# Query copies and probability scaling on GpSimd, with a re-fitted order table, in a recurrent memory transformer block

## The chip, the cores and the metric

The kernel runs on one core of one Trainium2 chip. The core has a TensorE (PE in the profile, with its weight loads listed apart as PEld), a VectorE (DVE), a ScalarE (ACT), a GpSimd (POOL) and a SyncE (SP) that issues the DMAs. The metric is the device time of one execution in microseconds; lower is better. The kernel before was timed three times.

## The reference

One block with two residual branches. The first is attention with 32 heads of 128 over segments of 32 tokens, in which every segment also carries 8 memory rows. The memory rows' output of a segment is the memory input of the next one, so the 64 segments form a chain. The second is a gelu MLP from 512 to 1792 and back.

```python
def _A_ref(x, mem0, Wq, Wk, Wv, Wo, seg_len):       # x: 2048 x 512
    mem = mem0                                      # 8 x 512
    for s in range(n_seg):                          # 64 segments, one after the other
        h = concat([mem, x[segment s]])             # 40 rows
        q, k, v = h @ Wq, h @ Wk, h @ Wv            # 32 heads of 128
        scores = (q @ k.T) * scale
        scores = where((idx[:, None] < M) | (idx[:, None] >= idx[None, :]), scores, -1e9)
        o = (softmax(scores) @ v) @ Wo
        mem = o[:M]                                 # the next segment needs it
        outs.append(o[M:])

h = x + _A_ref(_layernorm(x), mem0, Wq, Wk, Wv, Wo, 32)
out = h + gelu(_layernorm(_layernorm(h)) @ w1 + b1) @ w2 + b2
```

## The kernel before

**Recording and planning.** The kernel doesn't write its instructions in their final order. `build_kernel` records operations (`S.op`, `S.either`, `S.dma`) with what they read and write and with a duration. `Sched.schedule` then gives every operation a start by a table of costs: `HOP` is the time between the end of an operation and the start of one that depends on it, `OVERLAP` is how far two neighbours on an engine may overlap, `SWITCH` is the price of a change of the PE's tile mode. Each operation's rank is the longest path behind it, plus a number from the table `BONUS` (by the tile that it writes and the place of its segment). `S.either` leaves the engine open: the planner takes the engine that ends first. On DVE, ACT and POOL the start times so found fix the order of the instructions, and on these in-order engines everything waits behind an instruction that waits.

**The PE's own order** is written out by hand. `ORDERS` lists, for each place, which units of which part come when: `Q0.0.2` is units 0 and 1 of the part Q0. Places are a1 to a3 (the first segments), m0 to m3 (segments 4 to 59, by their number modulo 4, 14 of each) and z60 to z63. `TURNED` says which passes walk their four 128-column chunks backwards; two passes that meet on the same chunk keep the loaded weights (`matmul_kept`).

**One segment.** In the matrix products the segment's rows are the PE's weights (128 by 32, four of them side by side) and the big weight matrices stream past, 512 columns at a time. A *unit* is four such matmuls.

- K0, K1, Q0, Q1, V0, V1 (line 796, or 547 with kept weights): four units each. The number is the half of the heads. K and Q leave PSUM as `kq` (ACT or DVE, lines 814 and 815) and are transposed on DVE (line 839) into `KALL` and `QT`. `q_seg` then copies the memory rows' queries from `QT` into `ZC` (line 853), and `qb_fill` adds queries of the tokens' extra rows from `QTB` (line 861, POOL).
- SC0, SC1 (line 963): the scores of the memory rows, from `ZC` and `KALL`. Their softmax is `nmc` (maximum, DVE, line 972), `EC` (exponential, ACT, 976), `rsc` (DVE, 979), `PC` (scaling, DVE, 982), `PTC` (transpose, DVE, 983).
- PV0, PV1 (lines 994 and 998): the memory rows' probabilities times V, in another tile mode. PVA (line 1055): the same for the tokens of the segment before.
- SA (line 1025): the tokens' scores. Their softmax is `nma`, `SA`, exponential, `sma`, `rsa` (1035 to 1039), `PA` (scaling with `rsa`, DVE, line 1042), `PTA` (transpose, DVE, line 1044). PVA of the next segment needs `PTA`.
- WO (line 1083): the output product, eight units. Its result is transposed on DVE (`TT`, line 1095) and its memory rows are added into `hT` (line 1089), which Q, K and V of the next segment read. This is the recurrence.
- F0, F1: work that doesn't hang on the recurrence and fills the PE: K, Q and V of extra rows of later blocks (`hB`), in m3 the eight units of `wo_B` (line 1112), near the end the first part of the MLP. `warm` units (line 765) take their place in the first segments.

After segment 63 the MLP runs (lines 1451 and 1465), with `p2_res` on POOL (line 1190) and `p2_norm` on DVE (line 1184). `align` inserts idle weight loads (pads) so that every fourth segment starts at the same place of the PE's instruction stream.

The lines around the change, with their numbers in the profile:

## Time and profile before

| | |
|---|---|
| timed, median of 3 | 807.47 us (805.72 to 808.97) |
| profiled execution, from its first to its last instruction | 802.2 us |
| difference of the two, which the profile doesn't show | 5.3 us |
| PE busy | 775.9 us (97%) |
| DVE busy | 600.7 us (75%) |
| ACT busy | 558.0 us (70%) |
| POOL busy | 90.1 us (11%) |
| granted PE clock, mean | 0.998 |

The first 60 us load the weights (16 MB), the segments run from about 43 to 705 us, the MLP ends the program. PE matmuls overlap in the profile: each row has its own length, and four stand side by side in the array. What a unit costs is therefore read from the distance of its start to the next unit's start, and "busy" is an upper bound on it. "Idle before" of PEld is time in which no weights were loaded, which costs nothing while the matmuls in the array keep it full.

### The profile page before, as it was taken

To read this page: it belongs to the slowest core of one execution; us is meant where nothing else is said; L and a number is where in the kernel's file an instruction comes from. 1 tells how busy PE (TensorE), PEld (TensorE's weight loads), DVE (VectorE), ACT (ScalarE), POOL (GpSimd) and SP (SyncE) were. 2 spreads that over 40 slices of the span, in tenths; PEclk is the share of its full clock that TensorE was granted. 3 is DMA by queue.
4 is the path that set the end of the run, shared out by engine and by line. 5 is a ranking of instruction groups with operands and counts; after the bars stand their busy time and mean duration, and the time that the engine had idled before them with its cause. 6 is when DMAs were issued, how large, how long until landed. Compare 5 with 4: busy or idle time off the path is not lost.

```text
span 802.2 us, 46835 instructions
## 1 busy us (share of the span) xinstructions
PE 775.9 (97%) x21699; PEld 423.1 (53%) x20880; DVE 600.7 (75%) x1847; ACT 558.0 (70%) x1580; POOL 90.1 (11%) x211
## 2 busy tenths in 40 slices
PE   2899999999999999999999999999999999999998
PEld 1455555555555555555555555555555555644444
DVE  3277878888888888888888888888888888732311
ACT  1557777777777777777778777777777777773342
POOL 5022000010001010101010101000000000020700
PEclk9999999999999999999999999999999999999999
DMA  9961010201111121102010202010212112074300
GB/s 367 394 174 24 4 37 11 45 12 37 26 33 30 30 33 27 36 19 42 19 43 15 49 12 50 13 37 20 50 25 56 51 38 59 17 232 127 86 27 26
DMA packets 65555, 48.77 MB, mean 61 GB/s; under 512 B 28996, under 2 KB 63308, under 8 KB 63820
## 3 DMA queue, kind: packets, MB, share of 16 engines
q1 hardware_dynamic: 65024, 45.50, 20.3%
q8 instruction: 166, 2.72, 1.4%
q14 instruction: 33, 0.27, 0.1%
q10 hardware_dynamic: 332, 0.27, 0.1%
HBM read 31.08 MB, written 8.13 MB: 49 GB/s over the span
## 4 chain that ended last, share of the span: by engine, by line
PE 91%; DMA 3%; DVE 2%; ACT 1%; SPq 1%; issue 1%; POOL 0%; DVEq 0%; ACTq 0%
PE ps L796 43%; PE ps L1083 15%; PE ps L547 8%; PE quad L1465 6%; PE ps L1451 5%; DMA WQ<-in_A_Wq_dram 3%; PE ps L1112 3%; PE quad L994 3%; PE quad L1055 2%; PE ps L1025 2%; PE ps L1233 1%; PE ps L963 1%; PE quad L963 1%; SPq L708 1%; PE quad L998 1%
## 5 line engine op out<-in xcount | busy, mean ns | idle before, releaser
L1083 PE MATMUL ps<-WO,OT 128*32 128x256 bf16 x4224 | 140.6, 274 | 0.1
L796 PE MATMUL ps<-WQ,hT 128*32 128x512 bf16 x1864 | 131.6, 379 | 0.7 <-DVE hT L1089 0.5
L796 PE MATMUL ps<-WV,hT 128*32 128x512 bf16 x1364 | 125.2, 381 | 0.0
L796 PE MATMUL ps<-WK,hT 128*32 128x512 bf16 x1700 | 123.6, 380 | 0.1
L815 ACT ACTIVATE kq<-ps 128x512 bf16<-128x512 f32 x160 | 95.4, 597 | 32.3 <-PE ps L796 26.4
L1083 PEld LDWEIGHTS ps<-WO,OT 128*32 128x32 bf16 x4224 | 100.9, 96 | 26.5 <-ACT OT L814 5.5
L814 ACT CAST kq<-ps 128x512 bf16<-128x512 f32 x162 | 94.8, 585 | 19.9 <-PE ps L796 13.1
L814 ACT CAST OT<-quad 128x128 bf16<-128x128 f32 x191 | 84.4, 442 | 27.0 <-PE quad L998 18.8
L839 DVE STREAM_TRANSPOSE KALL<-kq 128x256 f32<-128x256 f32 x160 | 71.2, 445 | 15.0 <-ACT kq L814 11.8
L796 PEld LDWEIGHTS ps<-WQ,hT 128*32 128x32 bf16 x1864 | 50.3, 97 | 58.8 <-issue 19.0
L861 POOL COPY ZC<-QTB 128x256 bf16<-128x256 bf16 x64 | 25.6, 401 | 477.2 <-PE ps L963 455.7
L796 PEld LDWEIGHTS ps<-WK,hT 128*32 128x32 bf16 x1700 | 45.8, 96 | 56.9 <-issue 14.5
L547 PE MATMUL ps<-WV,hT 128*32 128x512 bf16 x684 | 67.6, 379 | 0.0
L796 PEld LDWEIGHTS ps<-WV,hT 128*32 128x32 bf16 x1364 | 38.4, 97 | 47.3 <-issue 36.6
L839 DVE STREAM_TRANSPOSE QT<-kq 128x256 f32<-128x256 f32 x128 | 57.0, 445 | 6.5 <-ACT kq L815 1.9
L1454 ACT ACTIVATE WQ<-ps,b1t 128x512 bf16<-128x512 f32 x42 | 28.9, 688 | 46.6 <-PE ps L1451 46.6
L1095 DVE STREAM_TRANSPOSE TT<-ps 128x256 f32<-128x256 f32 x66 | 29.7, 450 | 36.3 <-PE ps L1083 36.1
L814 ACT CAST VS<-ps 128x512 bf16<-128x512 f32 x65 | 38.1, 586 | 26.6 <-PE ps L796 26.5
L814 DVE CAST VS<-ps 128x512 bf16<-128x512 f32 x63 | 41.8, 663 | 5.4 <-PE ps L796 5.4
L1541 DVE TENSOR_TENSOR WV<-quad,WV 128x512 bf16<-128x512 f32 (+1 forms) x16 | 10.5, 672 | 45.6 <-PE quad L1465 45.6
L982 DVE TENSOR_TENSOR PC<-EC,rsc 128x128 bf16<-128x128 f32 x128 | 39.7, 310 | 4.3
L1112 PE MATMUL ps<-WO,OTB 128*32 128x512 bf16 x512 | 42.1, 381 | 0.4 <-issue 0.2
(163 smaller groups left out, 1432.1 us busy)
## 6 DMA issues: line engine op xcount, KB each, us to landing
WV<-in_A_Wv_dram SPq DMA_DIRECT2D x4, 1024.0 KB, 8.5
WK<-in_A_Wk_dram SPq DMA_DIRECT2D x4, 1024.0 KB, 14.2
WQ<-in_A_Wq_dram SPq DMA_DIRECT2D x4, 1024.0 KB, 24.7
WO<-in_A_Wo_dram SPq DMA_DIRECT2D x8, 512.0 KB, 9.4
v_last<-VSB SPq DMA_DIRECT2D x60, 64.0 KB, 2.9
VBD<-v_last SPq DMA_DIRECT2D x60, 64.0 KB, 2.9
h_mid<-xr SPq DMA_DIRECT2D x16, 128.0 KB, 1.8
WK<-in_B_w_dram SPq DMA_DIRECT2D x4, 512.0 KB, 4.6
```

What stands on the lines that cost most here:

```text
L547: return e.add_instruction(mybir.InstMatmult(name="I-%d" % (4000000 + _kept[0]), engine=mybir.EngineType.PE, start_tensor_calc=start, stop ...
L796: ins = e.matmul(o, l, m, start=(k == 0), stop=(k == DC - 1), tile_position=(0, 32 * j), skip_group_check=True)
L814: return {"act": (lambda e: e.copy(out, src), t_act(n, ps_)), "dve": (lambda e: e.tensor_copy(out, src), 0.16 + 1.042e-3 * n * fast)}
L815: return {"act": (lambda e: e.mul(out, src, scale_), t_act(n, ps_)), "dve": (lambda e: e.tensor_scalar(out, src, scale_, None, ALU.mult), ...
L839: S.op("dve", lambda e: e.transpose(out, src), reads=[("kq", i)], writes=[key], dur=t_dve(256) + 0.02, after=after)
L982: S.op("dve", lambda e: e.tensor_tensor(PC[:, r].rearrange("p t a -> p a t"), EC[:, r], bc, ALU.mult), reads=[("EC", r), ("rsc", r)], writ ...
L1083: ins = e.matmul(ps[bank][32 * j:32 * j + 32, 0:256], lhs(slot(h)), wo_cols(h, b), start=(k == 0), stop=(k == 15), tile_position=(0, 32 * ...
L1095: S.op("dve", lambda e: e.transpose(tt.rearrange("p c q t -> p (c q t)"), ps[bank][:, 0:256]), reads=[("ps", bank)], writes=[("TT", par)], ...
L1112: ins = e.matmul(ps[bank][32 * j:32 * j + 32, :], OTB[:, bk % 2, slot(h), :], WO[:, h, :], start=(k == 0), stop=(k == 7), tile_position=(0 ...
L1451: ins = e.matmul(ps[bank][:, 0:SBT], W1[:, cc, fc * P:(fc + 1) * P], hnT_of(k)[:, cc, :], start=(cc == 0), stop=(cc == DC - 1))
L1454: S.op("act", lambda e: e.activation(gT[:, fc, :], ps[bank][:, 0:SBT], ACTF.Gelu_apprx_tanh, bias=b1t[:, fc:fc + 1], scale=1.0), reads=[(" ...
L1465: S.op("pe", lambda e: e.matmul(quad[:, t, :], lhs, W2[:, fc, :], **flags), reads=[("W2", part_of(fc))] + gT_keys(k, fc), writes=[("ps", t ...
```

## The change

What it does:

1. `q_seg` copies the memory rows' queries on POOL. Before, the planner chose ACT or DVE for each.
2. The scaling of the tokens' probabilities (`PA`) may go to DVE or POOL.
3. The planner's costs are changed: waits between particular pairs of engines (`NEAR`), a charge when a PE unit waits for two engines that end close together (`TWICE`), neighbours marked `apart` that don't overlap (`ALONE`), and new durations.
4. A second reader of a PSUM bank on the engine that read it first no longer waits for the first reader's semaphore (`again`).
5. `BONUS`, `TURNED` and `ORDERS` hold new numbers.
6. In the last norm's preparation the variance is turned into `1.00001*var + 1e-10` in place of `var + 1e-5`, in the same one instruction.

```diff
-HOP = {"pe": 0.21, "act": 0.06, "dve": 0.05, "pool": 0.08, "sp": 2.0}
+HOP = {"pe": 0.215, "act": 0.052, "dve": 0.054, "pool": 0.08, "sp": 2.0}
+NEAR = {("act", "dve"): 0.032, ("dve", "act"): 0.034, ("act", "act"): 0.034, ("dve", "dve"): 0.034, ("pool", "pool"): 0.034}
+TWICE = 0.09
+ALONE = 0.031
...
-          "m0": "Q0.0.2 Q1.0.1 Q0.2.4 K0.0.4 Q1.1.4 K1.0.4 SC0.0.1 V0.0.1 V1.0.2 V0.1.2 V1.2.3 V0.2.4 SC1.0.1 V1.3.4 F0.0.1 PVA.0.2 PV0.0.1 F0.1.4 WO.0.2 PV1.0.1 WO.2.8 F1.0.4 SA.0.1",
+          "m0": "Q0.0.2 Q1.0.1 Q0.2.4 K0.0.4 Q1.1.2 K1.0.1 Q1.2.4 K1.1.4 SC0.0.1 V1.0.1 V0.0.2 V1.1.3 V0.2.4 SC1.0.1 F0.0.1 V1.3.4 PVA.0.2 PV0.0.1 F0.1.4 WO.0.2 PV1.0.1 WO.2.8 SA.0.1 F1.0.4",
...
-            if w is not None:
+            if w is not None and excl and k in w.reads and k not in w.writes:
+                again.add(w)
+            elif w is not None:
                 deps.add(w)
...
-                    t = max(t, q.start + q.dur + (SWITCH if q.mode != o.mode else 0.0))
+                    free = q.start + q.dur + (SWITCH if q.mode != o.mode else 0.0)
+                    t = max(t, free) + self.twice(o, t, free)
...
-                if p.eng == E and E not in self.self_sync:
+                if p.eng == E and (E not in self.self_sync or p in o.again):
                     continue
...
-            zc[r] = S.either({"act": (lambda e: e.copy(dst, src), 0.31), "dve": (lambda e: e.tensor_copy(dst, src), 0.25)}, reads=[("QT", r)],
+            zc[r] = S.either({"pool": (lambda e: e.tensor_copy(dst, src), 0.31)}, reads=[("QT", r)],
                              writes=[("ZCm", s % 2, r)])
...
-            S.op("dve", lambda e: e.tensor_tensor(PA[:].rearrange("p a t b -> p a b t"), SA[:].rearrange("p (a b) t -> p a b t", b=2), bc2, ALU.mult),
-                 ["SA", "rsa"], ["PA"], dur=0.418)
+            def pa(e):
+                return e.tensor_tensor(PA[:].rearrange("p a t b -> p a b t"), SA[:].rearrange("p (a b) t -> p a b t", b=2), bc2, ALU.mult)
+            S.either({"dve": (pa, 0.418), "pool": (pa, 0.7)}, reads=["SA", "rsa"], writes=["PA"])
...
-            S.op("pool", lambda e: e.tensor_scalar(rs, ag[:, 1:2], 1e-5, None, ALU.add), reads=[("ag2", bk)], writes=[("rs2", bk)], dur=0.2)
+            S.op("pool", lambda e: e.tensor_scalar(rs, ag[:, 1:2], 1.00001, 1e-10, ALU.mult, ALU.add), reads=[("ag2", bk)], writes=[("rs2", bk)], dur=0.2)
```

Counted over the whole program, all 128 copies of `ZC` from `QT` (64 on ACT and 64 on DVE before) and 62 of the 64 `PA` come to POOL. 11 of the mask copies into SA's bank (`maskAF`) move from ACT to DVE, and 2 casts of `VS` from DVE to ACT. The PE has the same matmuls; 1368 of them keep their weights instead of 1216, and 284 pads on `hT` stand in place of 230. The DMAs are the same.

How the instructions stand now, at three places. First DVE at the start of an m3 segment, from the end of the tokens' softmax of the segment before (`rsa`) to the scaling of the memory rows' probabilities (`PC`). Before:

```order
L1039 RECIPROCAL rsa<-sma 128x8
L839 STREAM_TRANSPOSE QT<-kq 128x256
L839 STREAM_TRANSPOSE KALL<-kq 128x256
L1042 TENSOR_TENSOR PA<-SA,rsa 128x4x2x32
L839 STREAM_TRANSPOSE QT<-kq 128x256
L972 TENSOR_REDUCE nmc<-quad 128x2
L853 COPY ZC<-QT 128x8x2x8
L839 STREAM_TRANSPOSE KALL<-kq 128x256
L1044 STREAM_TRANSPOSE PTA<-PA 128x128
L979 RECIPROCAL rsc<-smc 128x2
L982 TENSOR_TENSOR PC<-EC,rsc 128x2x64
```

The same place of the changed kernel:

```order
L1074 RECIPROCAL rsa<-sma 128x8
L874 STREAM_TRANSPOSE QT<-kq 128x256
L874 STREAM_TRANSPOSE KALL<-kq 128x256
L1080 STREAM_TRANSPOSE PTA<-PA 128x128
L874 STREAM_TRANSPOSE QT<-kq 128x256
L1007 TENSOR_REDUCE nmc<-quad 128x2
L874 STREAM_TRANSPOSE KALL<-kq 128x256
L1014 RECIPROCAL rsc<-smc 128x2
L1017 TENSOR_TENSOR PC<-EC,rsc 128x2x64
```

`PA` and the `ZC` copy are gone from DVE, and `PTA` stands where `PA` stood, two transposes behind `rsa` and ahead of the second `QT`; it waits for POOL. In the other places `PTA` stands behind the second `KALL`, as before. On POOL the rows from an m2 to an m3 segment are now as follows (before, only the copies from `QTB`, those from `xT` and the small norm instructions stood there):

```order
L888 COPY ZC<-QT 128x8x2x8
L1078 TENSOR_TENSOR PA<-SA,rsa 128x4x2x32
L888 COPY ZC<-QT 128x8x2x8
L896 COPY ZC<-QTB 128x16x2x8
L771 TENSOR_SCALAR rst<-agg 128x1
L772 TENSOR_TENSOR rst<-rst,cneg 128x1
L1078 TENSOR_TENSOR PA<-SA,rsa 128x4x2x32
L888 COPY ZC<-QT 128x8x2x8 x2
L896 COPY ZC<-QTB 128x16x2x8
```

Each segment has two copies from `QT`. In m2 (the first four rows), and likewise in m0 and m1, `PA` stands between them; in m3 (the last three rows) it stands ahead of both. Second, the PE in an m3 segment, from the second SC to the first Q units of the next segment. Before:

```order
L963 MATMUL ps<-KALL,ZC 32x64 x16
L1112 MATMUL ps<-WO,OTB 32x512 x4
L796 MATMUL ps<-WV,hT 32x512 x4
L1055 MATMUL quad<-PTA,VS 128x32 x32
L994 MATMUL quad<-PTC,VS 128x16 x16
L998 MATMUL quad<-PTC,VBD 128x64 x4
L1112 MATMUL ps<-WO,OTB 32x512 x16
L1083 MATMUL ps<-WO,OT 32x256 x8
L994 MATMUL quad<-PTC,VS 128x16 x16
L998 MATMUL quad<-PTC,VBD 128x64 x4
L1083 MATMUL ps<-WO,OT 32x256 x56
L1112 MATMUL ps<-WO,OTB 32x512 x8
```

Now:

```order
L998 MATMUL ps<-KALL,ZC 32x64 x16
L1148 MATMUL ps<-WO,OTB 32x512 x4
L831 MATMUL ps<-WV,hT 32x512 x4
L1091 MATMUL quad<-PTA,VS 128x32 x32
L1029 MATMUL quad<-PTC,VS 128x16 x16
L1033 MATMUL quad<-PTC,VBD 128x64 x4
L1148 MATMUL ps<-WO,OTB 32x512 x12
L1119 MATMUL ps<-WO,OT 32x256 x16
L1029 MATMUL quad<-PTC,VS 128x16 x16
L1033 MATMUL quad<-PTC,VBD 128x64 x4
L1119 MATMUL ps<-WO,OT 32x256 x48
L1148 MATMUL ps<-WO,OTB 32x512 x12
```

Behind the last WO unit stand three `wo_B` units (12 matmuls) and SA and then one more (before: two, SA and one more). In m0 the four F1 units stand behind SA now; before, SA was the last of the segment. Third, the PE in an m1 segment between SC1 and WO. Before:

```order
L963 MATMUL ps<-KALL,ZC 32x64 x16
L796 MATMUL ps<-WV,hT 32x512 x4
L796 MATMUL ps<-WQ,hB 32x512 x4
L1055 MATMUL quad<-PTA,VS 128x32 x32
L994 MATMUL quad<-PTC,VS 128x16 x16
L998 MATMUL quad<-PTC,VBD 128x64 x4
L796 MATMUL ps<-WQ,hB 32x512 x12
```

Now:

```order
L998 MATMUL ps<-KALL,ZC 32x64 x16
L831 MATMUL ps<-WV,hT 32x512 x4
L1091 MATMUL quad<-PTA,VS 128x32 x32
L831 MATMUL ps<-WV,hT 32x512 x4
L831 MATMUL ps<-WQ,hB 32x512 x4
L1029 MATMUL quad<-PTC,VS 128x16 x16
L1033 MATMUL quad<-PTC,VBD 128x64 x4
L831 MATMUL ps<-WQ,hB 32x512 x12
```

PVA and PV0, which stood next to each other, now have two units of 512 columns between them.

More of the change, by code (lines that the diff above doesn't have):

```diff
@@ L255, in lat, with over, twice @@
             return 0.0
-        return HOP[p.eng]
+        if p.eng == o.eng and p in o.again:
+            return -OVERLAP[p.eng]
+        return NEAR.get((p.eng, o.eng), HOP[p.eng])
+    @staticmethod
+    def over(p, o):
+        return -ALONE if p.apart or o.apart else OVERLAP[o.eng]
+    def twice(self, o, t, free):
+        if t <= free + 0.01:
+            return 0.0
+        last = {}
+        for d in o.deps:
+            if d.eng != "pe":
+                v = d.start + d.dur + self.lat(d, o)
+                k = "dma" if d.is_dma else d.eng
+                if k not in last or v > last[k][0]:
+                    last[k] = (v, d)
+        if len(last) < 2:
+            return 0.0
+        top = max(last.values(), key=lambda x: x[0])[1]
+        for k, (v, d) in last.items():
+            if d is not top and v + 0.1 > o.prev.start and not any(x.eng == d.eng and x.start >= d.start for x in top.deps if not x.is_dma):
+                return TWICE
+        return 0.0
     def schedule(self):
```

63 lines of the change are left out of this document (34 added, 29 removed), and 157 rows, old and new, of tables (BONUS, ORDERS).

## The prediction

> **What bounds the kernel now.** I read the page's head first, then the busy time of the long middle, then the waits there, then single segments in time order.
>
> ```profile
> span 802.2 us, 46835 instructions
> PE 775.9 (97%) x21699; PEld 423.1 (53%) x20880; DVE 600.7 (75%) x1847; ACT 558.0 (70%) x1580; POOL 90.1 (11%) x211
> PE 91%; DMA 3%; DVE 2%; ACT 1%; SPq 1%; issue 1%; POOL 0%; DVEq 0%; ACTq 0%
> ```
>
> The third line is the chain that ended last. The same for the segments alone, from 64 to 697 us (columns: window, length, busy PE, PEld, DVE, ACT, POOL with counts, granted PE clock, DMA share, GB/s), and the two waits that matter:
>
> ```profile
> 64.00:697.00 633.00, 630.94 (x20004) 350.63 (x19010) 541.90 (x1710) 483.81 (x1440) 52.20 (x132) 1.00 0.14 31
> ```
>
> ```profile
> DVE TT L1095 <- PE ps L1083: 31.0, 51, 2.2
> PEld ps L796 <- DVE hT L1089: 9.4, 30, 0.8
> ```
>
> The PE sets the pace (91% of the chain) at full clock, with the same matmuls before and after. So the time can change only where the PE stands still or changes its tile mode. DVE, 86% busy there (541.90/633.00), itself waits 31.0 us for WO at the start of the recurrence. Freeing DVE or ACT shortens no path by itself. I therefore cost the places where the order of the PE, or an instruction on the path, moves. "Class" is a place m0 to m3, 14 segments each.
>
> **A. End of m0.** These are PE and DVE in time order (start, length, engine and line, operation, tiles, count), first at the end of an m0, then of an m2 segment:
>
> ```profile
> 420.49 1.04 PE L796 MATMUL ps<-WK,hB 128*32 128x512 bf16 x16
> 421.72 0.40 PE L796 MATMUL ps<-WK,hT 128*32 128x512 bf16 x4
> ...
> 441.01 0.42 PE L1025 MATMUL ps<-KALL,QT 128*32 128x32 bf16 x32
> 442.16 0.40 PE L796 MATMUL ps<-WK,hT 128*32 128x512 bf16 x4
> ```
>
> ```profile
> 420.79 0.45 DVE L1095 STREAM_TRANSPOSE TT<-ps 128x256 f32<-128x256 f32 x1 [0.33 <-PE ps L1083]
> ...
> 441.24 0.45 DVE L1095 STREAM_TRANSPOSE TT<-ps 128x256 f32<-128x256 f32 x1 [0.47 <-PE ps L1083]
> ```
>
> From the first matmul behind WO to the first one on the new `hT` it takes 1.23 us in m0 and 1.15 in m2, though both put the same work there. `TT` starts 0.30 and 0.23 behind that first matmul. In the program the `TT` of m0 waits for two semaphores (PE, and DVE because `oBn` stands close ahead); the others wait for PE alone. In the changed kernel 1 of 12 such double waits is left. Gain: 12 x 0.07 = **-0.9 us** (bounds 0 and -0.9). That SA now stands ahead of F1 in m0 is free: the 1.15 is latency, and the four units and SA fit into it.
>
> **B. End of m3.** Here is the PE, at an end without and one with a stop:
>
> ```profile
> 451.43 0.60 PE L1112 MATMUL ps<-WO,OTB 128*32 128x512 bf16 x8
> 451.86 0.40 PE L1025 MATMUL ps<-KALL,QT 128*32 128x32 bf16 x32
> 452.09 0.41 PE L1112 MATMUL ps<-WO,OTB 128*32 128x512 bf16 x4
> 452.58 0.62 PE L796 MATMUL ps<-WQ,hT 128*32 128x512 bf16 x8
> ```
>
> ```profile
> 410.04 1.13 PE L1112 MATMUL ps<-WO,OTB 128*32 128x512 bf16 x8
> ...
> 411.43 0.84 PE L796 MATMUL ps<-WQ,hT 128*32 128x512 bf16 x12
> ```
>
> Two units take 0.43 (451.43 to 451.86), so a unit is 0.216. Three units and SA (0.23) are 0.88 of 1.15 us: 0.27 idle in front of Q. The change puts a fourth unit there, worth 14 x 0.216 = -3.0 us if that idle time were always free. It isn't: at 410.04 the first two units last 1.13 instead of 0.60, with no semaphore waited for, and the whole takes 1.39. The program's count of PE instructions puts a multiple of 256 inside this second unit, in every m3. Reading the 14 ends, 2 have no stop, 4 stop for about 0.15, 4 for 0.22 to 0.26, 4 for 0.35 to 0.53. With four units only 0.05 of cover is left, so the gain per end is 0.216, 0.11, 0.02 and 0: 0.43 + 0.44 + 0.07 = **-0.9 us** (bounds 0 and -3.0).
>
> [...]
>
> **C. Middle of m3.** The memory rows' probabilities, PE and then DVE (the last two PE rows are from an m2 segment):
>
> ```profile
> 445.63 0.30 PE L963 MATMUL quad<-KALL,ZC 128*32 128x64 bf16 x16
> ...
> 447.59 0.40 PE L796 MATMUL ps<-WV,hT 128*32 128x512 bf16 x4
> 447.93 0.37 PE L1055 MATMUL quad<-PTA,VS 32*128 32x32 bf16 x32
> 448.21 0.27 PE L994 MATMUL quad<-PTC,VS 32*128 32x16 bf16 x16
> ```
>
> ```profile
> 447.27 0.31 DVE L982 TENSOR_TENSOR PC<-EC,rsc 128x128 bf16<-128x128 f32 x1
> 447.64 0.29 DVE L972 TENSOR_REDUCE nmc<-ps 128x2 f32<-128x128 f32 x1
> 447.85 0.23 DVE L983 STREAM_TRANSPOSE PTC<-PC 128x64 f32<-128x64 f32 x1
> ```
>
> ```profile
> 437.92 0.37 PE L1055 MATMUL quad<-PTA,VS 32*128 32x32 bf16 x32
> 438.13 0.30 PE L994 MATMUL quad<-PTC,VS 32*128 32x16 bf16 x16
> ```
>
> SC0 starts at 445.63 and `PTC` ends at 448.08: 2.45 us. This length is pure latency, the same within 0.02 in m0, m1 and m3. PV0 follows PVA by 0.28 in m3 and by 0.21 in m2, so PV0 of m3 already waits 0.07 for `PTC`. Between SC0 and PV0 stand 9 units before, and 8 in the changed m3 (`V1.0` has gone ahead of SC0), with `nmc` still between `PC` and `PTC`. PV0 could then start 2.30 behind SC0, but `PTC` ends at 2.45, and the matmul needs about 0.06 more (0.13 now, from 448.08 to 448.21, less the 0.07 that a double wait costs in A), so it waits 0.21. That is 0.14 more than now, 14 times: **+2.0 us** (bounds: 0, if `PTC` comes sooner, and 14 x 0.216 = +3.0, if the double wait costs the same as now).
>
> **D. m1.** Between PVA and PV0 now stand two units. The PE changes mode once more each way: 447.59 to 447.93 is 0.34 where a unit takes 0.216, so 0.12 in, and back I take nothing (bound 0.12). In return PV0, with `PTC` now right behind `PC`, no longer waits its 0.07. Net 0.05 x 14 = **+0.7 us** (bounds -1.0 and +2.4). The stop in m1 falls behind WO:
>
> ```profile
> 140.56 1.29 PE L796 MATMUL ps<-WQ,hB 128*32 128x512 bf16 x12
> ...
> 142.11 0.62 PE L796 MATMUL ps<-WK,hT 128*32 128x512 bf16 x8
> ```
>
> This takes 1.55 instead of 1.15; over the 14 ends such stops cost 0.9 us. The count now puts the multiple of 256 at SA, a little later after the last one. I take half: **-0.5 us** (bounds 0 and -0.9).
>
> **E. z60 to z62.** Four fewer units stand behind WO, at most 4 x 0.216 = 0.9 us of cover lost. Part of them was more than the latency needs, so I take **+0.4** (bounds 0 and +0.9).
>
> **F. The copies and PA on POOL.**
>
> ```profile
> L853 ACT COPY ZC<-QT 128x128 bf16<-128x128 bf16 x64 | 19.2, 300 | 1.5 <-DVE QT L839 0.4
> L853 DVE COPY ZC<-QT 128x128 bf16<-128x128 bf16 x64 | 14.0, 219 | 0.1
> L1042 DVE TENSOR_TENSOR PA<-SA,rsa 128x256 bf16<-128x256 f32 x64 | 26.7, 418 | 0.1
> L861 POOL COPY ZC<-QTB 128x256 bf16<-128x256 bf16 x64 | 25.6, 401 | 477.2 <-PE ps L963 455.7
> L1190 POOL TENSOR_TENSOR WV<-WQ,b2bc 128x512 f32<-128x512 bf16 x16 | 18.1, 1169 | 37.2 <-DVE WV L1184 37.1
> ```
>
> DVE loses about 40 us and ACT 19, all beside the PE. POOL gets 128 copies, at most 0.40 each (the row with twice the elements), and 62 `PA`, which no row shows on POOL. Below it is bounded by 0.40 (256 elements, one input), above by 1.17 (512 elements, two inputs); half of the latter, 0.6, is nearest in kind. POOL sums to under 160 us of 802, so it can only be late, not full. The tightest place is the start of m3:
>
> ```profile
> 444.05 0.20 DVE L1039 RECIPROCAL rsa<-sma 128x8 f32<-128x8 f32 x1
> 445.17 0.42 DVE L1042 TENSOR_TENSOR PA<-SA,rsa 128x256 bf16<-128x256 f32 x1
> ```
>
> `PTA` now stands where `PA` stood, free to start at 445.17, and `rsa` ends at 444.25. With two handovers of about 0.1, `PA` may take 0.7. At 0.6 it is covered: **0** (the other end is rival 3). If it is late, the second `QT`, `nmc`, `KALL` and `PTC` wait behind `PTA` on DVE, and SC1 and PV0 behind them; the `ZC` copies wait behind `PA` on POOL.
>
> Sum: -0.9 - 0.9 + 2.0 + 0.7 - 0.5 + 0.4 = +0.8 us on a profiled 802.2 + 5.3 = 807.5 (the median is 807.47): **808.3 us**.
>
> **Rivals.**
>
> 1. *Faster: the new orders remove the remaining stalls.* The chain shows the same step of m0 four segments apart:
>
> ```profile
> 287.73 2.62 PE ps L796 x48
> ...
> 411.62 2.59 PE ps L796 x48
> ...
> 452.58 2.77 PE ps L796 x48
> ```
>
> Four segments take 41.30 on average up to 411.62 ((411.62 - 287.73)/3) and once 40.96, with the same work. If fewer late operands and stops bring each group to the best, 14 x 0.34 = -4.8, and with A another -0.9: 801.8. For it: DVE and ACT are freed by 59 us. Against it: C, and that the PE waits little for either.
>
> 2. *The double waits and stops cost as before and C is hidden:* 807.5, no effect.
>
> 3. *Slower: PTA waits for POOL in m3.* If `PA` takes 1.17 instead of the allowed 0.7, DVE stands 0.47 at `PTA`, and `PTC`, on which PV0 already waits, is as late: 14 x 0.47 = +6.6, with the sum 814.9. It decides from 0.7 us on.
>
> 4. *Slower: POOL and DVE get into each other's way.* `PC` on DVE, over the whole run (min, median and longest ns):
>
> ```profile
> L982 DVE TENSOR_TENSOR PC<-EC,rsc x128: 303/308/416, 41.2 to 697.2; 128x128 bf16<-128x128 f32 x128
> ```
>
> The longest, beside a POOL copy, lost 0.108. POOL is now busy three times as long; if one `PC` on the path of PV0 loses that in each of 60 segments, +6.5: 814.8. Against it: the median is 5 ns above the minimum, with POOL's old copies already there. [...]
>
> **How the numbers follow.** About 0.5%, 4 us, is what a measurement of this kernel can tell: the three runs spread over 3.3 us. Chances: forecast 0.42 (same), rival 1 0.28 (faster, if it comes in full), rival 2 0.12 (same), rival 3 0.09 and rival 4 0.05 (slower), and 0.04 left for a gain off these places. Rival 2 and the forecast lie within 803.4 to 811.5; of the forecast, 0.02 goes beyond on either side. So faster 0.28 + 0.04 + 0.02 = 0.34, same 0.38 + 0.12 = 0.50, slower 0.09 + 0.05 + 0.02 = 0.16. Likeliest alone: the larger bounds give 804 to 812. The range reaches to rival 1 and a little past it, and up to the forecast with C and D at their upper ends: 800 to 812.
>
> **What would show it.** A right if no end of m0 takes over 1.2 us from WO to Q; B if Q in m3 starts at once behind the fourth unit, with stops now in the open; C if PV0 follows PVA by 0.4 in m3; D by two more mode changes in m1; F if `PTA` in m3 never waits for POOL and `PA` takes under 0.7. The forecast is wrong if the groups of four segments come to 41.0 or less, or if `PA` takes 1 us.

## The result and the profile after

The changed kernel takes 819.88 us (median of 4 runs, 817.32 to 823.23) against 808.22 us (805.72 to 810.32) for the kernel before on the same chip. The ratio is 1.0165, with a 95% interval of 1.0138 to 1.0193. The change makes the kernel slower by 11.7 us in the medians; 808.3 us, in a range of 800 to 812, was forecast, so the median lies 7.9 us above the range.

Where the time and the span of an execution are both on record, the time is 1.7 to 2.0 us longer (here 817.32 and 815.6). So the 5.3 us between the median and the profile of the kernel before are not all time that a profile leaves out: the execution profiled there, with a span of 802.2 us, was some 3.5 us faster than the median of 807.47. The profile of the changed kernel is that of the fastest of its four executions.

The page's head for the profiled run: the span, the busy time of the engines, the queue that brings PE's instructions (packets, MB, share), and the chain that ended last.

```profile
span 815.6 us, 46805 instructions
PE 778.9 (96%) x21699; PEld 417.2 (51%) x20782; DVE 571.9 (70%) x1730; ACT 545.7 (67%) x1507; POOL 163.3 (20%) x401
...
q8 instruction: 166, 2.72, 1.4%
...
PE 90%; SPq 5%; DVE 2%; issue 1%; DMA 1%; ACT 1%; DVEq 0%
```

DVE has 29 us less to do (about 40 were forecast), ACT 12 less (19 were forecast), POOL 73 more, and the span is 13.4 us longer (815.6 - 802.2). PE still carries the chain. So time is lost where PE stands still, and that is read at the places of the prediction's terms.

**A, the end of m0.** PE in time order (start, length, line, operation, tiles, count):

```profile
427.25 0.42 PE L1060 MATMUL ps<-KALL,QT 128*32 128x32 bf16 x32
427.50 1.06 PE L831 MATMUL ps<-WK,hB 128*32 128x512 bf16 x16
428.40 0.40 PE L831 MATMUL ps<-WQ,hT 128*32 128x512 bf16 x4
```

From the first matmul behind WO to the first on the new `hT` it is now 1.15 us (428.40 - 427.25); it was 1.23. No end of m0 is longer.

**B, the end of m3.** First one without a stop, then one with:

```profile
627.68 0.82 PE L1148 MATMUL ps<-WO,OTB 128*32 128x512 bf16 x12
628.33 0.40 PE L1060 MATMUL ps<-KALL,QT 128*32 128x32 bf16 x32
628.55 0.41 PE L1148 MATMUL ps<-WO,OTB 128*32 128x512 bf16 x4
628.83 1.26 PE L831 MATMUL ps<-WQ,hT 128*32 128x512 bf16 x20
```

```profile
246.18 0.82 PE L1148 MATMUL ps<-WO,OTB 128*32 128x512 bf16 x11
247.79 0.38 PE L1148 MATMUL ps<-WO,OTB 128*32 128x512 bf16 x1 [0.79 <-issue]
```

At 627.68 four units and SA take the same 1.15 us that three units and SA took before: the moved unit costs nothing there. At 246.18 PE halts ahead of the last matmul of the third unit, with no semaphore to wait for ("issue"), for about a microsecond.

**The end of m1.** The same kind of halt, now behind the second matmul of SA:

```profile
350.87 1.51 PE L1119 MATMUL ps<-WO,OT 128*32 128x256 bf16 x48
352.20 0.18 PE L1060 MATMUL ps<-KALL,QT 128*32 128x32 bf16 x2
353.59 0.37 PE L1060 MATMUL ps<-KALL,QT 128*32 128x32 bf16 x30 [1.21 <-issue]
```

**C, the middle of m3**, PE and DVE:

```profile
454.05 0.30 PE L998 MATMUL quad<-KALL,ZC 128*32 128x64 bf16 x16
...
455.47 0.31 PE L998 MATMUL ps<-KALL,ZC 128*32 128x64 bf16 x16
...
456.15 0.37 PE L1091 MATMUL quad<-PTA,VS 32*128 32x32 bf16 x32
456.46 0.27 PE L1029 MATMUL quad<-PTC,VS 32*128 32x16 bf16 x16
```

```profile
455.67 0.31 DVE L1017 TENSOR_TENSOR PC<-EC,rsc 128x128 bf16<-128x128 f32 x1
455.88 0.28 DVE L1007 TENSOR_REDUCE nmc<-ps 128x2 f32<-128x128 f32 x1
456.08 0.23 DVE L1018 STREAM_TRANSPOSE PTC<-PC 128x64 f32<-128x64 f32 x1
```

And SC1 in the m3 segment of the kernel before that the prediction shows:

```profile
447.25 0.31 PE L963 MATMUL ps<-KALL,ZC 128*32 128x64 bf16 x16
```

`PTC` ends 2.26 us behind SC0 (456.31 - 454.05), no longer 2.45, and PV0 follows PVA by 0.31, hardly more than before (0.28). The reason is in the rows of SC1 and `nmc`. `nmc` of the second half stands on DVE between `PC` and `PTC` and reads what SC1 writes. Before, SC1 began 1.62 us behind SC0 (447.25 - 445.63), and `nmc` 0.39 behind SC1, when `PC` had been over for 0.06. Now a unit fewer stands between SC0 and SC1, which begins 1.42 behind SC0 (455.47 - 454.05); `nmc` follows `PC` at once, and `PTC` comes 0.19 sooner. So the 2.45 us held a wait for the PE's own order.

**D, the middle of m1**, on four engines:

```profile
433.73 0.37 PE L1091 MATMUL quad<-PTA,VS 32*128 32x32 bf16 x32
434.03 0.40 PE L831 MATMUL ps<-WV,hT 128*32 128x512 bf16 x4
...
434.57 0.27 PE L1029 MATMUL quad<-PTC,VS 32*128 32x16 bf16 x16
...
434.81 0.83 PE L831 MATMUL ps<-WQ,hB 128*32 128x512 bf16 x12
435.71 0.62 PE L1119 MATMUL ps<-WO,OT 128*32 128x256 bf16 x16
```

```profile
433.67 0.40 POOL L896 COPY ZC<-QTB 128x256 bf16<-128x256 bf16 x1 [1.01 <-PE ps L998]
```

```profile
433.70 0.52 DVE L1017 TENSOR_TENSOR PC<-EC,rsc 128x128 bf16<-128x128 f32 x1
434.26 0.25 DVE L1018 STREAM_TRANSPOSE PTC<-PC 128x64 f32<-128x64 f32 x1
434.43 0.25 DVE L1007 TENSOR_REDUCE nmc<-ps 128x2 f32<-128x128 f32 x1
```

```profile
434.72 0.31 ACT L1011 ACTIVATE EC<-ps,nmc 128x64 f32<-128x64 f32 x1 [0.29 <-DVE nmc L1007]
...
435.31 0.26 ACT L849 CAST OT<-quad 128x128 bf16<-128x128 f32 x1
```

POOL's copy for the block rows begins 0.03 us ahead of `PC` on DVE, and `PC` takes 0.52 us instead of 0.31. `PTC`, `nmc` and `EC` move back in their turn; the cast `OT` stands behind `EC` on ACT; and WO, which needs `OT`, begins 0.90 us behind the three units at 434.81, where these take 0.65. PE stands still for about 0.24 us, in each of the 14 m1 segments. The copy came first here, and `PC` lost 0.21 us. In an m2 segment, too, the copy begins first, by 0.18 us, on POOL and DVE:

```profile
445.31 0.40 POOL L896 COPY ZC<-QTB 128x256 bf16<-128x256 bf16 x1 [0.80 <-PE ps L998]
```

```profile
445.49 0.38 DVE L1017 TENSOR_TENSOR PC<-EC,rsc 128x128 bf16<-128x128 f32 x1
```

In this run 35 of the 128 `PC` take over 0.33 us, and every one of them ends 0.15 to 0.16 us behind the end of a POOL copy that began ahead of it. A copy that begins behind `PC`, even by 0.04 us, leaves `PC` at 0.32 us or less (33 cases). In these 68 cases it came down to which of the two began first, and how long the copy then still ran.

**F, the new work on POOL**, by source line (durations in ns: min, median, longest), and who waited for it:

```profile
L1078 POOL TENSOR_TENSOR PA<-SA,rsa x62: 617/619/658, 45.2 to 716.0; 128x256 bf16<-128x256 f32 x62
...
  DVE PTA L1080: 0.4, 1
```

`PA` takes 0.62 us (0.6 was assumed), and DVE waited for it once, for 0.4 us.

**What the halts are.** PE and PEld have 21,699 + 20,782 = 42,481 instructions, and the queue "instruction" q8 brought 166 packets of 16 KB: 255.9 instructions for each. The program counts in blocks of 256, and the multiples of 256 in B and D of the prediction are their boundaries. By this count, the stop at 352.20 falls on instruction 4 of SA, the fourth (two weight loads, two matmuls) being the last of its block, and the stop at 246.18 falls on the seventh of the third unit's eight. In the trace, each of the 148 blocks so counted between 64 and 690 us has the start of one packet in it. For the stop at 352.20 the boundary before it was passed at 348.26, the packet began at 350.95, ended at 352.24, and PE went on at 353.59. At the boundaries of these 148 blocks there are 16 stretches of 0.24 us or more in which no matmul and no weight load begins, and each of them ends 1.26 to 1.55 us behind the end of the packet that began in the block before (in the kernel before 13 of 0.23 us or more, 1.24 to 1.64 us behind). So here PE stopped where a packet began late and the block then running ended early.

The next table is worked out from the matmul records of 56 segments (14 of each class). "End" is the time from the last WO matmul of a segment to the first projection of the next on its `hT`, over the shortest value, 1.253 us, summed over 14. "Middle" is the whole stretch from the last WO matmul of the segment before to the last of this one, summed, less the same in the kernel before; that of m1 begins with the end of m0, so it also holds term A.

| us | end m0 | middle m1 | end m1 | middle m3 | end m3 |
|---|---|---|---|---|---|
| before | 1.0 | 0 | 0.9 | 0 | 0.8 |
| after | 0.0 | +4.6 | 5.6 | -2.7 | 5.3 |

So m1 became longer, m3 shorter as B meant it, and the halts at two ends grew from 1.7 to 10.9 us.

### The profile page after: what moved, and what is told of

It reads as the page before. It is cut to its first block, busy times and chain, and to the rows that moved or that the text cites. A ratio compares the mean times of both kernels' runs of the same rounds, so it can differ in the third digit from the quotient of the medians.

```text
span 815.6 us, 46805 instructions
## 1 busy us (share of the span) xinstructions
PE 778.9 (96%) x21699; PEld 417.2 (51%) x20782; DVE 571.9 (70%) x1730; ACT 545.7 (67%) x1507; POOL 163.3 (20%) x401
## 4 chain that ended last, share of the span: by engine, by line
PE 90%; SPq 5%; DVE 2%; issue 1%; DMA 1%; ACT 1%; DVEq 0%
PE ps L831 40%; PE ps L1119 15%; PE ps L582 9%; PE quad L1501 6%; PE ps L1487 5%; PE ps L1148 4%; SPq L757 3%; PE quad L1029 3%; PE quad L1091 2%; PE ps L1060 2%; PE ps L1269 1%; DMA WO<-in_A_Wo_dram 1%; SPq L743 1%; PE ps L998 1%; PE quad L998 1%
## 5 line engine op out<-in xcount | busy, mean ns | idle before, releaser
L831 PE MATMUL ps<-WK,hT 128*32 128x512 bf16 x1688 | 125.7, 379 | 0.1
L849 ACT CAST OT<-quad 128x128 bf16<-128x128 f32 (+1 forms) x191 | 85.8, 449 | 28.3 <-PE quad L1033 26.6
L888 POOL COPY ZC<-QT 128x128 bf16<-128x128 bf16 x128 | 37.6, 294 | 305.9 <-DVE QT L874 305.0
L1078 POOL TENSOR_TENSOR PA<-SA,rsa 128x256 bf16<-128x256 f32 x62 | 38.4, 620 | 104.6 <-DVE rsa L1074 104.6
L831 PEld LDWEIGHTS ps<-WV,hT 128*32 128x32 bf16 x1344 | 35.8, 96 | 36.6 <-issue 20.0
L1017 DVE TENSOR_TENSOR PC<-EC,rsc 128x128 bf16<-128x128 f32 x128 | 44.6, 349 | 3.8
```

The lines of the kernel that those rows point to most:

```text
L831: ins = e.matmul(o, l, m, start=(k == 0), stop=(k == DC - 1), tile_position=(0, 32 * j), skip_group_check=True)
L849: return {"act": (lambda e: e.copy(out, src), t_act(n, ps_)), "dve": (lambda e: e.tensor_copy(out, src), 0.16 + 1.042e-3 * n * fast)}
L888: zc[r] = S.either({"pool": (lambda e: e.tensor_copy(dst, src), 0.31)}, reads=[("QT", r)], writes=[("ZCm", s % 2, r)])
L1017: S.op("dve", lambda e: e.tensor_tensor(PC[:, r].rearrange("p t a -> p a t"), EC[:, r], bc, ALU.mult), reads=[("EC", r), ("rsc", r)], writ ...
L1078: return e.tensor_tensor(PA[:].rearrange("p a t b -> p a b t"), SA[:].rearrange("p (a b) t -> p a b t", b=2), bc2, ALU.mult)
```

## The experiments

Theory 1 of the first four runs: the lost time is in the new orders, in m1 and in what they do to the fetching of PE's instructions, and not in the work on POOL. Theory 2, the rival: the work on POOL costs it, by contention or by being late. All numbers of "end" and "middle" below are as in the table above.

**1. The old tables with the new engines.**

```diff
-BONUS, TURNED, ORDERS of the changed kernel
+BONUS, TURNED, ORDERS of the kernel before
```

> The changed kernel with the three tables BONUS, TURNED and ORDERS of the kernel before; the copies and PA stay on POOL and the new costs stay. Theory 1 (the new order of the PE lets the places at which the PE needs the next 256 instructions fall where they come too late, and costs 0.33 us in each m1): the stops at the ends of m1 and m3, 10.9 us in the changed kernel against 1.6 us before, go back to about 2 us and m1 loses its 0.33; 806 to 811 us, PA on POOL stays at 0.62. [...]

Measured: 807.04 us, a ratio of 1.0007 (0.9991 to 1.0022). The whole loss goes with the tables: under the old orders, where `PC` takes 0.310 us on average as in the kernel before (0.349 in the changed kernel), POOL's work costs nothing, and the 29 us that DVE is spared bring nothing either. Ends: 0.9 in m0 (A's double wait is back), 2.6 in m1, 0.5 in m3.

**2. The new tables with the old engines.**

```diff
-            zc[r] = S.either({"pool": (lambda e: e.tensor_copy(dst, src), 0.31)}, reads=[("QT", r)],
+            zc[r] = S.either({"act": (lambda e: e.copy(dst, src), 0.31), "dve": (lambda e: e.tensor_copy(dst, src), 0.25)}, reads=[("QT", r)],
...
-            S.either({"dve": (pa, 0.418), "pool": (pa, 0.7)}, reads=["SA", "rsa"], writes=["PA"])
+            S.either({"dve": (pa, 0.418)}, reads=["SA", "rsa"], writes=["PA"])
```

> The changed kernel with the copies of ZC from QT on ACT or DVE and PA on DVE, as before; the new tables and costs stay. Theory 1: the PE order is the same, so the stops at the ends of m1 and m3 stay, 7 to 12 us together; 815 to 822 us. Theory 2: 806 to 811 us.

Measured: 880.23 us, ratio 1.0915 (1.0880 to 1.0951). Both expectations are far off. m1 and m3 become longer by about 2 us each; it seems that the new orders leave DVE no room for work that it no longer had when they were made. The run can't say what the orders alone are worth.

**3. Only the order of PE in m1 put back.**

```diff
-          "m1": "Q0.0.1 K0.0.2 Q0.1.4 Q1.0.1 K0.2.4 ... SC1.0.1 V0.3.4 PVA.0.2 V1.3.4 F0.0.1 PV0.0.1 F0.1.4 ... SA.0.1 F1.0.4",
+          "m1": "K0.0.1 Q0.0.2 K0.1.2 Q0.2.4 K0.2.3 ... SC1.0.1 V1.3.4 F0.0.1 PVA.0.2 PV0.0.1 F0.1.4 ... F1.0.3 SA.0.1 F1.3.4",
```

> The changed kernel with only the PE order of m1 as before (PVA and PV0 side by side, SA behind three units). Theory 1: the 0.33 us in each of 14 m1 goes (-4.6 us), and the stops at the end of m1 (5.5 us in the changed kernel) become about 1 to 3 us, since the next block is needed at the second unit behind WO again; those of m3 stay: 810 to 814 us. Theory 2: 817 to 821 us, as the work on POOL is the same.

Measured: 825.27 us, ratio 1.0252 (1.0193 to 1.0311): slower than the changed kernel, which neither theory gave. The stops at the end of m1 go (0.3 us), as expected. But the middle of m1 grows to +7.9, probably because DVE and ACT keep priorities made for the other order (run 8 puts these back as well, and the middle with them), and the ends of m3 go to 7.6, where the blocks now begin at another instruction.

**4. Only `PA` back on DVE.**

```diff
-            S.either({"dve": (pa, 0.418), "pool": (pa, 0.7)}, reads=["SA", "rsa"], writes=["PA"])
+            S.either({"dve": (pa, 0.418)}, reads=["SA", "rsa"], writes=["PA"])
```

> The changed kernel with PA on DVE alone; the ZC copies stay on POOL. Theory 1: 816 to 821 us, stops as in the changed kernel. Theory 2, in the form that PA (0.62 us) keeps the copies behind it waiting: 810 to 814 us.

Measured: 832.22 us, ratio 1.0320 (1.0283 to 1.0358). Again neither: m1 is longer by 1.6 us a segment than in the kernel before. As in 2, an order fitted to one placement doesn't bear the other.

**5. The copy for the block rows held behind `PC`.**

```diff
+            S.op("pool", ... writes=[("ZCb", par)], dur=0.45, after=[pc[0]])
...
+            pc[r] = S.op("dve", lambda e: e.tensor_tensor(PC[:, r]...
```

> The changed kernel, with the copy of the block rows' queries (ZCb) held behind the product PC of column half 0 of the segment before, so that it cannot stand beside that product. Theory 1 (in m1 the copy that begins just ahead of PC makes PC .525 us instead of .31, and with it nmc, EC1, the cast OT and WO late by .24 us): PC is .30 to .32 us in all m1 segments, the gap between the projection and WO falls from .445 to about .21 us, the steady loss of m1 from .33 to about .1 us in 14 segments, 816 to 817.5 us. Theory 2 (WO is late by the new order on VectorE and ScalarE, whatever PC takes): PC shorter, the gap of .445 us stays, 819 to 821 us.

DVE, POOL and PE at the place shown for D:

```profile
433.22 0.30 DVE L1017 TENSOR_TENSOR PC<-EC,rsc 128x128 bf16<-128x128 f32 x1
```

```profile
433.65 0.40 POOL L896 COPY ZC<-QTB 128x256 bf16<-128x256 bf16 x1 [1.48 <-DVE PC L1017]
```

```profile
434.34 0.83 PE L831 MATMUL ps<-WQ,hB 128*32 128x512 bf16 x12
435.02 0.62 PE L1119 MATMUL ps<-WO,OT 128*32 128x256 bf16 x16
```

`PC` is back at 0.30 us, WO begins 0.68 us behind the three units instead of 0.90, and the middle of m1 falls from +4.6 to +1.4 us: so the copy beside `PC` costs 3.1 us in the middle of m1, and the mechanism of theory 1 is right. Yet the time is 819.1 us, a ratio of 1.0156 (1.0138 to 1.0174), which is theory 2's time and no gain that can be told from the changed kernel. The end of m1 now costs 7.1 us instead of 5.6. The wait that was taken away lies inside the block that ends at SA, and a block that is passed sooner would meet its late successor sooner. One profile doesn't show that, though: run 13 has a larger difference with no edit at all.

**6. All block boundaries 16 instructions further on.**

```diff
-LOCK = 106
+LOCK = 90
```

> The changed kernel with the start of each group of four segments set 16 instructions further on in TensorE's blocks of 256 (LOCK 90 instead of 106), so that every boundary falls 16 instructions later in the order; nothing else moves. Theory 1 (the stops at SA in m1 and at the third unit behind WO in m3 are TensorE's wait for its next block of 256 instructions): both places lose their stops; they come back some 16 instructions into SA, in m1 and in m3, and new ones arise at PV1 in m0 and m2, whose blocks now last 3.3 us instead of 3.8 us (by .3 to .8 us in each of 29 segments); 825 to 840 us. Theory 2 (the stops belong to what is done there, a bank or a semaphore that the records don't show): the stops stay at the first matmul of SA and at the third unit, 818 to 822 us.

PE at an end of m1 and at an end of m3:

```profile
569.50 0.23 PE L1060 MATMUL ps<-KALL,QT 128*32 128x32 bf16 x10
571.20 0.32 PE L1060 MATMUL ps<-KALL,QT 128*32 128x32 bf16 x22 [1.46 <-issue]
```

```profile
293.43 0.21 PE L1060 MATMUL ps<-KALL,QT 128*32 128x32 bf16 x7
294.42 0.33 PE L1060 MATMUL ps<-KALL,QT 128*32 128x32 bf16 x25 [0.78 <-issue]
```

In m1 the stop has moved from behind 2 matmuls of SA to behind 10: 8 matmuls and 8 weight loads are 16 instructions. In m3 it has left the third unit and stands behind 7 matmuls of SA. This shows that the halts are block boundaries and belong to nothing that is done at the place. The time is 822.97 us (ratio 1.0206, 1.0173 to 1.0238), less than theory 1 gave. The block that ends in SA of m1 is about 0.3 us shorter, 4 us in 14 segments, and its stops are 4.9 us longer (10.5 against 5.6); run 13 shows 3.4 us of difference at this end without any edit, so that the two come close proves little. The new stops expected at PV1 in m0 and m2 did not come, though the blocks there are as short as 3.3 us; two others came, at PV0 in m3.

**7. The new tables in m0 and m3 alone, on the kernel of 1.**

```diff
 ORDERS, TURNED and the "@m0" and "@m3" entries of BONUS
-as in the kernel before
+as in the changed kernel
```

> The kernel of the run with the tables of before (copies and PA on GpSimd, 807.0 us), with the changed kernel's orders, directions and priorities in m0 and m3 alone: the places of terms A and B by themselves, m1 and m2 as before. Theory 1 (A and B gain as forecast, but the block that begins at PV0 in m3 ends at the third unit behind WO, and TensorE stops there as in the changed kernel): -.07 us in each m0 and -.17 us in each m3, 14 of each, -3.4 us in all, and 2.5 to 5.5 us of stops at the end of m3: 806 to 809 us. Theory 2 (the stops come from elsewhere, from what m1's new order has made late): no stops at the end of m3, 803 to 805 us.

Measured: 810.73 us, ratio 1.0051 (1.0033 to 1.0069), above theory 1's range by 1.7 us, far from theory 2. The middle of m3 is 3.0 us shorter and the end of m0 1.0, both of the size expected, and the ends of m3 cost 5.1 us though m1 is as before. Against run 1 another 1.3 us are lost ahead of segment 4 and 2.9 us from segment 60 on, where the tables are the old ones; that is more than the 1.7 us by which the range is missed, and its cause is open.

**8. m1's tables alone put back in the changed kernel.**

```diff
 ORDERS["m1"], TURNED["m1"] and the "@m1" entries of BONUS
-as in the changed kernel
+as in the kernel before
```

> The changed kernel with the orders, directions and priorities of before in m1 alone (the run that put back only the order of TensorE there kept the new priorities for VectorE and ScalarE). Theory 1 (m1's loss is its whole set of tables: .33 us a segment and the stops at SA): m1's steady loss is under .1 us and its stops fall from 5.5 us to about 1 us; the boundary in m3 then lies at the fifth instruction of SA, as with the order of TensorE alone, and the stops there are 5 to 7.5 us: 809 to 813 us. Theory 2 (the priorities do nothing that the order does not): as with the order of TensorE alone, 823 to 827 us.

Measured: 813.83 us, ratio 1.0083 (1.0065 to 1.0102): theory 1, though 0.8 us above its range. The middle of m1 is back at -0.8 (A's gain), its ends at 2.6 (about 1 was expected), and the ends of m3 cost 7.5 us. Read against 3, which put back only PE's order, the priorities and directions count as much.

**9. m0's tables alone, on the kernel of 1.**

```diff
 ORDERS["m0"], TURNED["m0"] and the "@m0" entries of BONUS
-as in the kernel before
+as in the changed kernel
```

> The kernel of the run with the tables of before (copies and PA on GpSimd), with the changed kernel's orders, directions and priorities in m0 alone: term A by itself. Theory 1 (A takes the double wait of TT out of m0 and touches no block of TensorE's instructions that ends too soon): the end of m0 1.25 us instead of 1.33, stops at the end of m1 and m3 no larger than before; 805 to 807.5 us, a ratio of .997 to 1.001. Theory 2 (every one of the new tables costs more in stops than it gains): 809 us or more, as with m0 and m3 together.

DVE and then PE in an m0 segment of this run:

```profile
297.50 0.68 DVE L1077 TENSOR_TENSOR oBn<-OTB 32x512 bf16<-32x512 f32 x1
...
298.49 0.49 DVE L938 TENSOR_TENSOR PC<-EC,rsc 128x128 bf16<-128x128 f32 x1
...
299.09 0.68 DVE L770 CAST VS<-ps 128x512 bf16<-128x512 f32 x1
299.68 0.23 DVE L939 STREAM_TRANSPOSE PTC<-PC 128x64 f32<-128x64 f32 x1
```

```profile
300.06 0.27 PE L950 MATMUL quad<-PTC,VS 32*128 32x16 bf16 x16 [1.00 <-DVE PTC L939]
```

Measured: 828.64 us, ratio 1.0260 (1.0236 to 1.0284). Neither theory: the ends of m0, m1 and m3 cost 2.7, 4.2 and 0.7 us, but most of the loss is elsewhere: PV0 waits 1.00 us here, and m0 is about as much longer in nearly every group of four, because `oBn`, which was recorded in m3 and has m3's old priority, now stands ahead of `PC`, and the cast `VS` (0.68 us) ahead of `PTC`. A class's tables can't be taken alone, since work of one segment runs in the next, and A by itself isn't shown by this run.

**10. The unit of B put back.**

```diff
-... PVA.0.2 PV0.0.1 F1.1.4 WO.0.2 PV1.0.1 WO.2.8 F1.4.7 SA.0.1 F1.7.8
+... PVA.0.2 PV0.0.1 F1.1.5 WO.0.2 PV1.0.1 WO.2.8 F1.5.7 SA.0.1 F1.7.8
```

> The changed kernel with one unit of m3 put back from behind WO to ahead of it (term B undone, all else as changed; the block from PV0 to the third unit behind PV1 keeps its instructions). Theory 1 (the stops at the end of m3 are the wait for that block, whatever stands in it): the .17 us that each m3 saves goes (+2.4 us in 14), and most of it is taken out of the stops, which begin as much later: 3 to 5 us of stops left, 818.5 to 822 us. Theory 2 (the unit behind WO is what makes the stops): stops under 1 us, 816 to 818 us.

PE at the end of an m3 segment:

```profile
455.98 0.60 PE L1148 MATMUL ps<-WO,OTB 128*32 128x512 bf16 x8
456.41 0.40 PE L1060 MATMUL ps<-KALL,QT 128*32 128x32 bf16 x32
456.63 0.41 PE L1148 MATMUL ps<-WO,OTB 128*32 128x512 bf16 x4
457.14 0.62 PE L831 MATMUL ps<-WQ,hT 128*32 128x512 bf16 x8
```

Measured: 812.44 us, ratio 1.0061 (1.0042 to 1.0080). Theory 2 holds, and the time is 3.6 us below its range. The middle of m3 is 2.6 us longer again, 0.19 each, and the ends of m3 fall from 5.3 to 0.3 us. A part of what is left is hidden: between 456.63 and 457.14 there is idle time again that a short stop can use. But most is that the stops themselves are smaller: with what is hidden they come to 1.2 us in run 10 and 6.0 in the changed kernel (3.4 in the kernel before), because the packets come sooner. In m3 they begin more than 1.6 us behind their boundary in 5 of 14 segments of the changed kernel and 1 of 14 here, though DVE, ACT and POOL have the same order. The stops of m1, where nothing was changed, are smaller too (2.4 against 5.6); run 13 shows how far that can be chance.

**11 and 12. Blocks 6 instructions earlier, without and with the copy held back.**

```diff
-LOCK = 106
+LOCK = 112
```

> The changed kernel with TensorE's blocks of 256 instructions beginning 6 instructions earlier in the order (LOCK 112 instead of 106), nothing else moved. In m1 the boundary comes to instruction 24 of PVA's second half instead of 30, in m3 to 27 of PVA's second half instead of the wait ahead of PV0: about where the kernel before and the run with its tables have them. In the eleven profiles so far 36 fetches began from .3 us before PV1's first matmul to .2 us after it and 60 in the .2 us behind that. Theory 1 (a fetch that has not begun before PV1's dense run of 40 instructions in .24 us waits it out; what makes the stops is how far ahead of PV1 a block begins, not how long it lasts): the fetches in m1 begin 1.1 us after the boundary instead of 1.6 to 2.7, in m3 at most two of 14 later than 1.5 us; the stops fall from 5.5 and 5.3 us to under 2 us each: 811 to 814.5 us. Theory 2 (the shorter the block, the longer the stop; m3's block now lasts 3.56 us instead of 3.68, m0's 3.65 instead of 3.77): stops as large or larger, 820 to 824 us.

> The run with the copy ZCb held behind PC, and in addition TensorE's blocks 6 instructions earlier as in the run sent beside it. Theory 1 (the loss is PC's .22 us in each m1, 3.1 us, and the stops, which hang on where the blocks begin, 8 to 9 us): both go, 807 to 811 us, 2.5 to 4 us less than the run sent beside it; the kernel is then about as fast as before. Theory 2 (the time saved ahead of a late block is swallowed by its stop wherever the block begins): no more than 1 us less than the run sent beside it.

Measured: 817.05 us, ratio 1.0125 (1.0099 to 1.0151), and 817.78 us, ratio 1.0151 (1.0125 to 1.0177). Theory 1 of the first falls. In m1 most packets still begin 1.5 to 1.7 us behind the boundary, and in m3 five of 14 later than 1.6. Only the very late ones in m1, over 2 us, fell, from 4 to 1. Of the second, theory 2 is the nearer one: the 3.1 us saved in m1 do not come out as time.

**13. The changed kernel once more.** No edit; a second profile of the same instructions.

> The changed kernel as it is, once more, for a second profile of the same instructions. Theory 1 (which fetch begins late is settled by the order around the block's boundary, segment for segment the same way): the stops lie in the same segments with the same lengths within .1 us. Theory 2 (the order sets only how many begin late, and which ones is chance): stops at the end of m1 and of m3 of 3 to 8 us each, in other segments than in the first profile; that would also be the spread of 817 to 823 us among the runs of one kernel.

The wait at SA (total, times, longest) of the changed kernel, and then the span and the same wait of this run, whose time is 824.06 us:

```profile
PEld ps L1060 <- issue: 14.0, 18, 1.4
```

```profile
span 822.3 us, 46786 instructions
...
PEld ps L1060 <- issue: 20.8, 21, 1.7
```

The span is 6.7 us longer (822.3 - 815.6), with the same middle of m1 (+4.5). The ends of m1 cost 8.9 us and those of m3 7.0 (3 to 8 each by theory 2), partly in other segments than the first time: of the four m1 segments whose packet began over 2 us late, three are late again, one isn't, and four others are. So which packet is late is not settled by the instructions, and within one execution, too, the 14 segments of a class differ. It may be most of the spread between the executions of one kernel. A difference of 2 or 3 us in the ends between two profiles is therefore no finding by itself.

**14. Blocks 16 instructions earlier.**

```diff
-LOCK = 106
+LOCK = 122
```

> The changed kernel with TensorE's blocks 16 instructions earlier (LOCK 122). So far, fetches of the block that holds PV1 that began more than 1.45 us after their boundary in m3: 9 of 14 with the blocks 16 later, 5 of 14 as changed, 5 of 14 with them 6 earlier; more than 2 us in m1: 8, 4 and 1. Theory 1 (how far ahead of PV1 a block begins sets how many are late): at most 2 of 14 late in m3 and none in m1, and since m3's block lasts 3.35 us, short stops of .1 to .4 us in most m3. Theory 2 (it does not): 4 or more late in m3, with stops over 1 us. In both the blocks of m0 and m2 behind PV1 last 3.4 to 3.5 us instead of 3.8, which may cost of its own; 815 to 830 us.

A single time: 819.87 us. Three of 14 packets are late in m3 (by the 1.45 us of the expectation) and two over 2 us in m1: between the two theories, which gave at most 2 and none, or 4 and more. The distance to PV1 may have a part, but it doesn't settle it.

**15. The unit of B put back and the copy held behind `PC`.**

> The changed kernel with both single causes mended that a run has shown: the unit of m3 put back ahead of WO (812.4 us alone) and the copy ZCb held behind PC (819.1 us alone). Theory 1 (they are independent: 7.5 us from the first, 3.1 us of shorter m1 from the second, of which the stops at the end of m1 may take some back): 808 to 812 us, a ratio of 1.002 to 1.006 to before. Theory 2 (what is saved ahead of m1's block is lost in its stop, as in the run of the copy alone): 812 to 814 us.

Its edits are those of 5 and 10 together. Measured: 811.36 us, ratio 1.0058 (1.0036 to 1.0081), in theory 1's range, but with no gain that can be told from 10 alone. The middle of m1 is 3.3 us shorter (+1.4 against +4.7), and its ends 2.5 us longer (4.9 against 2.4). The copy was held back in three pairs of runs (5 against the changed kernel, 12 against 11, 15 against 10). In none did the time fall by more than the noise, though m1's middle became 2.2 to 3.3 us shorter in each profile. That fits a saving that the stop at m1's end takes back, but since the stops differ by as much by chance, it isn't shown. The ends of m3 stay at 0.3 us.

No run beats the kernel before; run 1 is level with it.

**What stays open** is why a packet begins later in one order than in another. Put together, the m3 packets that began more than 1.6 us behind their boundary were 3 of 56 with four units between PV0 and WO (before, 1, 10 and 15) and 37 of 70 with three (after, 13, 5, 7 and 8). Some of these blocks begin up to some ten instructions apart, but in 10 nothing but the unit is moved. So the moved unit makes them late, by run 10 and by these counts. How it does so isn't shown. Nor do the runs settle why the packets of m1's changed order begin later (10 of 14 over 1.6 us behind the boundary, 1 of 14 before). In eleven profiles 36 packets began from 0.3 us before PV1's first matmul to 0.2 us after it and 60 in the 0.2 us behind that (the expectation of 11), but 11 and 14 show that this isn't a rule to steer by.

## Why the prediction was wrong, step by step

- **A, -0.9: right.** The ends of m0 went from 1.0 to 0.0 us over the shortest value.
- **B, -0.9 with bounds of 0 and -3.0: the step that failed.** The unit itself brought nearly what its full bound said: putting it back cost 2.6 us. The prediction also named the stop in that place, and that cover shrinks to 0.05. But it carried over the stops of the kernel before ("2 have no stop, 4 stop for about 0.15, ..."), 3.4 us with what is hidden, as if the unit left them alone. By its sum 2.9 us would then stand open at the m3 ends (0.8 + 3.0 - 0.9). Measured are 5.3 us open, up to 1.1 us each, and 6.0 with what is hidden; with the unit put back it is 0.3 open and 1.2 in all. So the unit made the stops larger, and net, B costs instead of gaining: the ratio falls from 1.0165 to 1.0061 without it. Of these 8 us, the profiles have 2.4 at the m3 ends and middle (5.0 - 2.6) and 3.2 in m1's smaller stops in run 10, which may be chance; and the changed kernel's profile is of an execution 2.6 us faster than its median.
- **C, +2.0: wrong, near 0.** `PTC` was taken to end 2.45 us behind SC0, as a pure latency. It ends at 2.26, because that length held `nmc`'s wait for SC1, and SC1 comes a unit sooner in the new order. PV0 follows PVA by 0.32 on average, where 0.35 was measured before (0.29 without the one at 158.1 us, where PE stopped) and 0.42 forecast.
- **D, +0.7 for the body of m1: wrong by size and by mechanism.** The middle of m1 costs +5.6 (the +4.6 of the table and A's 1.0, which lies in the same stretch). Of this 3.1 us is the copy beside `PC`, shown by 5, which the prediction had as rival 4. The other 2.5 us, 0.18 in each m1, fit the extra mode change (0.12 in, and now something back), but no run separates that. And the 3.1 us did not come out as time when they were taken away (5, 12, 15).
- **D, -0.5 for the stop of m1: wrong in sign.** It was argued that a boundary "at SA, a little later after the last one" makes the stop smaller. The stops at the end of m1 went from 0.9 to 5.6 us. The block did become longer (about 3.95 us without a stop, 3.4 before). That doesn't help when its packet begins later: 10 of the 14 packets here began over 1.6 us behind the boundary, 4 of them over 2 us; before, it was 1 of 14. Why is open.
- **E, +0.4: about right.** From segment 60 on another 0.6 us is lost.
- **F, 0: right**, but for `PC` in m1. Run 1 has all of POOL's new work at a ratio of 1.0007. The sum of POOL's work, "under 160 us", was too low even by its own terms (90.1 + 128 x 0.40 + 62 x 0.6 is 178); 163.3 us was measured, 1.8 times as much as before and not three times. Nothing hung on it.

Sum of the profile: -1.0 (A) + 5.6 (m1) + 4.7 (5.6 - 0.9, end of m1) - 2.7 (m3) + 4.6 (5.3 - 0.8, end of m3) + 0.6 (E) = 11.8 of 13.4 us; m2's middle, 0.10 us longer in each, has most of the rest.

Of the rivals, 3 fell (0.4 us in all). Rival 4 was right that POOL's copies lengthen `PC`, and its price was mis-sized: 0.21 us and not 0.108, on the path in 14 segments and not 60. Only in m1 does the copy begin just ahead of `PC`; in m2 it begins earlier, and `PC` takes 0.38 us; in m0 and m3 it begins 0.21 to 0.26 us behind the first half's `PC`, which keeps its 0.30 to 0.31. (Six `PC` of the second half in m3 are lengthened by POOL's copies from `xT`.) It gave 814.8 for +6.5; it accounts for 3.1. What carried the chances astray is that the stops, though seen, were no rival. The quoted row at 410.04 alone showed 0.5 us at one end; a case in which every m3 stops as long behind a full cover is 7 us. The 14 ends that were read show what the old order gave, and nothing showed that a new order would keep it.

## What to carry to other kernels

On a kernel whose PE is busy 96% of the span, a new order has to be costed at the boundaries of its instruction blocks too: count the instructions, look at what lies between two boundaries, and treat a stop seen there as a quantity that can grow (here from 1.7 to 10.9 us at two places), not as a constant. An order, its priorities and the placement of work are fitted to each other: four of the runs that changed one alone (2, 3, 4 and 9) were slower than both kernels, 3 only just. When work moves between engines, look also at what it then runs beside: here a POOL copy that began 0.03 us ahead of `PC` on DVE made it 0.21 us longer. Holding that copy back brought no time that could be measured (runs 5, 12 and 15). And a latency read from a trace (the 2.45 us of C) may hold a wait for the very order that is changed: follow it instruction by instruction before it is carried over.
